# Two more column tiles as seven block products, with block sums made by GpSimd

## The chip, the cores and the metric

The kernel runs on one core of a Trainium2 chip. The metric is the device time of one execution in microseconds (us); less is better. TensorE is called PE here, VectorE DVE, ScalarE ACT, GpSimd POOL and SyncE SP, as in the profile.

## What is computed

Attention with a soft cap on its scores (2 batches, 12 heads, 448 positions, head size 64), and behind it two feed-forward blocks on 896 tokens of 768 numbers:

```python
x = _moe_ref(x=x, **moe_kwargs)      # h = x @ w_in; h * softmax(h), normalised, @ w_out
# and the second block, which the change is about:
g = x @ w_gate                       # 768 -> 1536
silu = g * (1.0 / (1.0 + np.exp(-g)))
val = x @ w_val                      # 768 -> 1536
return (silu * val @ w_out).astype(np.float32)
```

All is float32. TensorE multiplies rounded parts: each matrix is split into hi (rounded) and lo (the rest), and a product is three matmuls, hi x hi, hi x lo and lo x hi (`mm3`). The split is one ACT copy (hi) and one DVE subtraction (lo); a split of a bank in PSUM reads that bank twice.

## The kernel before

The stages follow each other on TensorE: attention, h (first block's first product), x (its second product, `ff1_x2`), the gate and value products (`ff2_gv`, `ff2_gv_seven`), and the output product (`ff2_out`).

The x stage makes six columns j of 128 model features for 896 tokens. Columns 0 and 1 are made in token blocks of 384, 256 and 256, columns 2 to 5 in blocks of 384 and 512. Each block's PSUM bank is split into `self.x2[j]` (hi and lo), and copied by ACT once more, as float32, into `self.xf` (line 582). Beside it w_out is converted column by column in two halves (`load_w_out`, lines 553 to 563): a DMA brings 64-bit raw words, ACT takes the absolute value, DVE clamps, shifts and merges in four steps, ACT scales by g_ln in four steps and makes hi, DVE makes lo. The first three steps of a half (absolute value, clamp, shift) are held in program order. Three w_out columns, two raw buffers and two float32 buffers exist at a time.

The gate and value stage runs over 12 column tiles fc of 128 features. A plain tile (`ff2_gv`) makes gate and value for 384 and then 512 tokens, 72 matmuls in all. A seven-product tile (`ff2_gv_seven`) takes gate and value weights, halved along the model features, as the four blocks of a 2 x 2 matrix, x halved along features and tokens as the other, and makes the product in seven block products of nine matmuls 448 wide in place of eight: 63 matmuls. It needs sums of weight blocks (`sum_steps`: two on POOL, two on DVE, and their splits) and sums of x blocks (`x_sums`, T1 to T4, split into `self.T`). Before, tiles 2 to 5 are of this kind (line 1036); `x_sums` runs in tiles 0 and 1, one of its four sums behind each half (line 1058), a subtraction 1344 wide on DVE and a split.

In a seven-product tile the products are, in order: A11 (bank g), S2 with T2 (b), A12 (on top of g), S3 with T3 (on top of b), S1 with T1 (c), A22 with T4 (e), S4 (on top of c). ACT copies bank g to `p1` after the first product, and the third may write g only after that. At the end come the multiplications of the results with silu, and `S1f`, `S3f`, `A11` and `A61`, which the output stage reads (lines 706 to 712).

Weights are kept in four buffers `self.g4` and in `self.w1`; plain tiles use two of them in turn. Raw loads go out on SP's queue, with two raw and two float32 buffers in the `st` pool. TensorE keeps program order throughout; from the x stage to the end of the gate and value stage the other engines' instructions are ordered by a planner when the kernel is built, and PE's are pinned. `early` (line 1034) says in which tile which part of the second w_out is loaded.

Of the kernel before, what the change touches and what calls it, by code (L numbers as in the profile page):

```python
# [5 lines left out]
F32 = mybir.dt.float32  # L6
# [4 lines left out]
AF = mybir.ActivationFunctionType  # L11
ALU = mybir.AluOpType
# [25 lines left out]
class Kernel:  # L38
# [526 lines left out]
    def ff1_x2(self, j, get, N, o):  # L565

        st = {}

        def part(a, z):
            def f():  # L570
                l, w = get(), self.wos[j]
                if a == 0:
                    st["ps"] = self.pt.tile([128, 512], F32, name=f"x2_{j}_{o}", tag="m")[:, :N]
                ps = st["ps"]
                for fc in range(a, z):
                    self.mm3(ps, (w[:, 0, fc, :], w[:, 1, fc, :]), (l[:, fc, 0, :], l[:, fc, 1, :]),
                             fc == 0, fc == self.K1 - 1)
                if z == self.K1:
                    hi, lo = self.x2[j][:, 0, o:o + N], self.x2[j][:, 1, o:o + N]
                    self.hi_act(hi, ps)  # L580
                    self.lo_dve(lo, ps, hi)
                    self.A.activation(self.xf[:, j, o:o + N], ps, AF.Copy)
            return (3 * (z - a) * N / 2400, f)

        c = self.K1 // 2
        return [part(0, c), part(c, self.K1)]


    def load_gv(self, fc, i):

        if fc not in self.gvs:
            self.gvs[fc] = [self.g4[(fc % 2) * 2 + n].rearrange("p (u k f) -> p u k f", u=2, f=128) for n in range(2)]
        n, w, d = "gv"[i], (self.w_gate, self.w_val)[i], self.gvs[fc][i]
        src = w[:, fc * 128:(fc + 1) * 128].rearrange("(k p) f -> p k f", p=128)
        f = self.f32_shifted(self.load_shifted(src, f"w{n}_{fc}"), f"w{n}_{fc}").rearrange("p (k f) -> p k f", k=self.KD)
        self.hi_act(d[:, 0], f)
        self.lo_dve(d[:, 1], f, d[:, 0])
# [24 lines left out]

    def x_sums(self, i):

        x = [self.xf[:, 3 * (m // 2):3 * (m // 2) + 3, 448 * (m % 2):448 * (m % 2) + 448] for m in range(4)]
        d, p, m, t = ((0, 1, 0, 0), (1, 3, 1, 2), (3, 3, 0, 1), (2, 2, 3, 3))[i]
        self.V.tensor_tensor(x[d], x[p], x[m], op=ALU.subtract)
        self.split([self.T[t][:, u] for u in range(2)], x[d])

    def sum_steps(self, fc):  # L630

# [29 lines left out]
    def ff2_gv_seven(self, fc):  # L661

        V, add, mult = self.V, ALU.add, ALU.mult
        n, k, ee = self.HN, fc, self.ee
        a, s24, s31, a22 = self.gvs[fc]
        half = lambda t, h: t.rearrange("p (h u k f) -> p h u k f", h=2, u=2, k=3)[:, h]
        A11, A12, S2, S4, S3, S1 = (half(t, h) for t in (a, s24, s31) for h in range(2))
        A22 = a22.rearrange("p u (k f) -> p u k f", k=3)
        X = lambda kh, th: [[self.x2[3 * kh + c][:, u, 448 * th:448 * th + 448] for u in range(2)] for c in range(3)]
        T1, T2, T3, T4 = ([[t[:, u, c] for u in range(2)] for c in range(3)] for t in self.T)  # L670
        bank = lambda m: self.pt.tile([128, 512], F32, name=f"{m}_{fc}", tag="m")[:, :448]

        def product(acc, w, x, start):
            for c in range(3):
                self.mm3(acc, (w[:, 0, c], w[:, 1, c]), x[c], start and c == 0, c == 2, not start)

        sg, c22, p1, u2 = (ee[:, 448 * m:448 * m + 448] for m in range(4))
        last = fc + 1 == self.KD
        first, second, third = (lambda: None,) * 3 if last else self.sum_steps(fc + 1)
        if last:  # L680
            self.load_gv(fc + 1, 1)
        a = bank("g")
        product(a, A11, X(0, 0), True)
        self.A.activation(p1, a, AF.Copy)
        b = bank("b")
        product(b, S2, T2, True)
        V.tensor_tensor(u2, p1, b, op=add)
        product(a, A12, X(1, 0), False)
        self.A.activation(sg, a, AF.Silu)
        first()  # L690
        if last:
            self.load_gv(fc + 1, 0)
        product(b, S3, T3, False)
        V.tensor_tensor(p1, p1, b, op=add)
        c = bank("c")
        product(c, S1, T1, True)
        V.tensor_tensor(c22, p1, c, op=add)
        second()
        e = bank("e")
        product(e, A22, T4, True)  # L700
        V.tensor_tensor(p1, p1, e, op=add)
        third()
        product(c, S4, X(1, 1), False)
        V.tensor_tensor(u2, u2, c, op=add)
        self.A.activation(u2, u2, AF.Silu)
        V.tensor_tensor(p1[:, :n], p1[:, :n], sg[:, :n], op=mult)
        V.tensor_tensor(self.S1f[:, k, :64], p1[:, n:], sg[:, n:], op=mult)
        self.split(self.A11[k], p1[:, :n])
        V.tensor_tensor(self.S1f[:, k, 64:], c22[:, :320], u2[:, :320], op=mult)
        V.tensor_tensor(c22[:, 320:], c22[:, 320:], u2[:, 320:], op=mult)  # L710
        V.tensor_tensor(self.S3f[:, k], p1[:, :n], self.S1f[:, k], op=ALU.subtract)
        self.split(self.A61[k], c22[:, 320:])

    def split(self, d, src):
# [212 lines left out]
    def run(self):  # L927
        nc = self.nc
        KD, K1, K2, F1 = self.KD, self.K1, self.K2, self.F1
# [16 lines left out]
        w = [self.w_in_steps(i) for i in range(KD)]  # L946
        f, g, hi, lo = zip(*w)
# [47 lines left out]
        n = self.HN = self.DM // 2  # L995
# [35 lines left out]
        self.sg = (self.ee[:, :n], self.ee[:, n:n + 512])  # L1031
        self.T1f = [self.ee[:, n + 512 + n * i:n + 512 + n * (i + 1)] for i in range(3)] + [t1, self.sms]
        self.t1 = t1
        early = {6: (6, 8), 7: (0, 1), 8: (2, 3), 9: (4,)}
        for fc in range(K2):
            if 2 <= fc < KD:
                self.ff2_gv_seven(fc)
                continue
            if fc == KD:
                w8 = self.w8 = wb.tile([128, 8, 2, n], F32R, name="w8", tag="w8")  # L1040
                w = both(w8) + [(w1[:, 0], w1[:, 1])]
                w += [p for g in self.g4[:2] for p in both(g.rearrange("p (k u n) -> p k u n", k=2, u=2))]
                self.B11, self.B21 = w[4:10], w[:4] + w[10:12]
            for i, (N, o) in enumerate(((n, 0), (512, n))):
                if fc == 1:
                    if i == 0:
                        first, second, third = self.sum_steps(2)
                        first()
                elif fc + 1 < K2:
                    self.load_gv(fc + 1, i)  # L1050
                elif i == 0:
                    self.load_w2(5)
                    self.load_w2(10)
                for c in early.get(fc, ())[i:i + 1]:
                    self.load_w2(c)
                self.ff2_gv(fc, N, o)
                if fc < 2:
                    self.x_sums(2 * fc + i)
            if fc == 1:
                second()  # L1060
                third()


        self.pinned = None
# [42 lines left out]
```

## Time and profile before

| | us |
|---|---|
| median of 3 runs (486.08 to 486.86) | 486.66 |
| the profiled execution | 486.02 |
| its span | 484.2 |
| PE busy | 474.9 |
| DVE busy | 371.7 |
| ACT busy | 303.3 |
| POOL busy | 29.5 |

The span is the time from the first to the last instruction that the profile shows; the execution's own time is 1.8 us longer. Matmuls are pipelined, so that rows of consecutive ones overlap by some tenths of a microsecond: the distance from one row's start to the next one's is the time that it costs. A note in square brackets is the idle time of the engine ahead of an instruction, and what ended it.

### The profile page before, as it was taken

Reading aid. Unit: us, or ns where it says so; the run is one execution under the profiler, and the core shown is the slowest. Engines: PE = TensorE matmul, PEld = TensorE weight load, DVE = VectorE, ACT = ScalarE, POOL = GpSimd, SP = SyncE. Lnnn points to the kernel's source line nnn. Section 1 sums busy time; section 2 is a strip of 40 time slices with the busy share of each in tenths; the row PEclk is TensorE's granted clock in tenths of the full one; section 3 lists DMA queues with packets and bytes.
Section 4 is the critical chain, followed back from the end, with each engine's and each line's share of the span. In section 5 each row is a group of like instructions: output and inputs, shape, how many; then the busy total and the mean of one; then the engine's idle time right before and its main releaser. Section 6 shows DMA issues by size and latency. Waiting matters only on the chain.

```text
span 484.2 us, 7694 instructions
## 1 busy us (share of the span) xinstructions
PE 474.9 (98%) x3006; PEld 390.4 (81%) x3006; DVE 371.7 (77%) x626; ACT 303.3 (63%) x440; POOL 29.5 (6%) x70
## 2 busy tenths in 40 slices
PE   9999999999999997999999999999999999999997
PEld 7445454548888897988998988899988899999996
DVE  3689999986779976475798878877567526999991
ACT  5999999931244787558976666777677616335220
POOL 1020101031000000000003011000000000000000
PEclk9999999999999998999999999999999999999999
DMA  6886565002001214126444234665566601010012
GB/s 184 206 209 153 123 174 146 20 2 87 1 0 43 88 45 111 65 72 208 131 130 137 72 119 130 195 195 186 168 231 197 195 1 49 17 57 10 18 53 93
DMA packets 65060, 52.34 MB, mean 108 GB/s; under 512 B 35584, under 2 KB 61952, under 8 KB 64256
## 3 DMA queue, kind: packets, MB, share of 16 engines
q1 hardware_dynamic: 64992, 51.86, 36.2%
q8 instruction: 23, 0.38, 0.3%
q14 instruction: 13, 0.11, 0.1%
q0 software_dynamic: 32, 0.00, 0.0%
HBM read 49.10 MB, written 2.75 MB: 107 GB/s over the span
## 4 chain that ended last, share of the span: by engine, by line
PE 93%; DVE 4%; ACT 2%; issue 1%; ACTq 0%
PE p L30 16%; PE g L30 14%; PE h L30 12%; PE v L30 12%; PE x L30 12%; PE pv L30 8%; PE sc L30 7%; PE S L30 4%; PE b L30 2%; PE c L30 2%; PE lt L30 1%; PE T L30 1%; PE warm L30 1%; DVE wo L30 1%; PE e L30 1%
## 5 line engine op out<-in xcount | busy, mean ns | idle before, releaser
L30 PE MATMUL g<-x,g 128*128 128x384 f32 (+2 forms) x360 | 77.0, 365 | 1.7 <-ACT ee L30 1.7
L30 PEld LDWEIGHTS g<-x,g 128*128 128x128 f32 x360 | 65.6, 188 | 9.8 <-ACT ee L30 2.8
L30 PE MATMUL v<-x,g 128*128 128x512 f32 (+1 forms) x288 | 60.2, 362 | 0.0
L30 PE MATMUL h<-wi,x 128*128 128x512 f32 x252 | 59.2, 393 | 0.0
L30 PEld LDWEIGHTS v<-x,g 128*128 128x128 f32 x288 | 52.1, 188 | 5.6
L30 PEld LDWEIGHTS h<-wi,x 128*128 128x128 f32 x252 | 46.8, 188 | 11.2 <-issue 1.5
L30 ACT ACTIVATE P<-sc,consts 112x896 f32<-112x896 f32 x48 | 45.3, 1009 | 3.8 <-PE sc L30 2.2
L30 ACT ACTIVATE P<-P,consts 112x3584 f32<-112x3584 f32 (+1 forms) x13 | 39.7, 3061 | 0.1
L30 PE MATMUL pv<-P,v 112*32 112x448 f32 x384 | 38.5, 540 | 0.0
L30 PEld LDWEIGHTS sc<-ks 64*112 64x112 f32 x288 | 23.3, 171 | 18.3 <-issue 8.4
L30 PE MATMUL sc<-ks 64*112 64x448 f32 x288 | 35.9, 379 | 0.2
L30 PE MATMUL x<-lB,wo 128*128 128x256 f32 (+1 forms) x192 | 35.2, 337 | 0.0
L30 PE MATMUL x<-lA,wo 128*128 128x384 f32 x144 | 29.5, 354 | 3.2 <-ACT wo L30 2.9
L30 PEld LDWEIGHTS x<-lB,wo 128*128 128x128 f32 x192 | 29.6, 189 | 3.4
L30 PEld LDWEIGHTS pv<-P,v 112*32 112x32 f32 x384 | 12.2, 110 | 22.9 <-issue 20.9
L30 PEld LDWEIGHTS x<-lA,wo 128*128 128x128 f32 x144 | 26.4, 198 | 5.0 <-ACT wo L30 3.4
L30 ACT ACTIVATE ee<-h,sms 128x512 f32<-128x512 f32 x14 | 9.5, 681 | 33.2 <-DVE sms L30 33.2
L30 PE MATMUL p<-w,a 128*128 128x384 f32 x144 | 26.8, 334 | 0.0
L30 PEld LDWEIGHTS p<-w,a 128*128 128x128 f32 x144 | 25.2, 188 | 0.1
L30 DVE TENSOR_TENSOR x<-x,x 128x448 fp32r<-128x448 f32 (+3 forms) x26 | 15.3, 587 | 10.6 <-ACT x L30 10.1
L30 DVE TENSOR_TENSOR g<-wg,g 128x768 fp32r<-128x768 f32 x16 | 15.3, 956 | 10.0 <-ACT g L30 9.3
L30 PE MATMUL S<-P,ones 112*32 112x448 f32 x192 | 22.4, 549 | 0.0
(201 smaller groups left out, 857.5 us busy)
## 6 DMA issues: line engine op xcount, KB each, us to landing
wg_raw<-in_moe_w_gate_dram SPq DMA_DIRECT2D x12, 765.8 KB, 4.2
wv_raw<-in_moe_w_val_dram SPq DMA_DIRECT2D x12, 765.8 KB, 4.2
wi_raw<-in_moe_w_in_dram SPq DMA_DIRECT2D x6, 1024.0 KB, 5.6
wo_raw<-in_moe_w_out_dram SPq DMA_DIRECT2D x12, 512.0 KB, 3.4
w_raw<-in_moe_w_out_dram SPq DMA_DIRECT2D x6, 767.6 KB, 4.2
v<-in_v_dram SPq DMA_DIRECT2D x24, 112.0 KB, 3.7
kq<-in_k_dram SPq DMA_DIRECT2D x22, 112.0 KB, 2.8
kq<-in_q_dram SPq DMA_DIRECT2D x22, 112.0 KB, 2.8
```

The lines of the kernel that those rows point to most:

```text
L30: i = f(*a, **k)
```

## The change

Tiles 1 to 6 are made as seven products in place of tiles 2 to 5. Tile 6 is the first whose results go on top of those of the first six (`A12`, `A22`, added to `S1f`), so its end is written out separately. Since tile 1 needs the x sums, they are made earlier: ACT no longer copies x's banks to `xf`; POOL adds hi and lo of a column when the column is complete (from column 2 on, which does columns 0 to 2), and makes the four block sums in pieces of 448, three for column 2 and three for each of columns 3 to 5. The splits (`x_split`) all run in tile 0, as do the weight sums of tile 1. In the tail of a seven-product tile the first product with silu is written to `S3f` rather than in place, and the 128-wide multiplication and S3's subtraction go to POOL. Tile 0 uses other weight buffers, tile 7's gate weight is loaded two products later within the last seven-product tile, and the loads of `early` and the `w8` buffer come one tile later.

```diff
@@ ff1_x2
-                    self.A.activation(self.xf[:, j, o:o + N], ps, AF.Copy)
+                    if o + N == 896 and j > 1:
+                        for m in range(3) if j == 2 else (j,):
+                            x = self.x2[m].bitcast(F32)
+                            self.G.tensor_tensor(self.xf[:, m], x[:, 0], x[:, 1], op=ALU.add)
+                        self.x_sums(j - 2)
@@ load_gv
-            self.gvs[fc] = [self.g4[(fc % 2) * 2 + n].rearrange("p (u k f) -> p u k f", u=2, f=128) for n in range(2)]
+            self.gvs[fc] = [self.g4[m].rearrange("p (u k f) -> p u k f", u=2, f=128)
+                            for m in (((0, 1), (2, 3))[fc % 2] if fc else (2, 1))]
@@ x_sums
-        x = [self.xf[:, 3 * (m // 2):3 * (m // 2) + 3, 448 * (m % 2):448 * (m % 2) + 448] for m in range(4)]
-        d, p, m, t = ((0, 1, 0, 0), (1, 3, 1, 2), (3, 3, 0, 1), (2, 2, 3, 3))[i]
-        self.V.tensor_tensor(x[d], x[p], x[m], op=ALU.subtract)
-        self.split([self.T[t][:, u] for u in range(2)], x[d])
+        c = i - 1
+        x = [self.xf[:, k + 3 * (m // 2), 448 * (m % 2):448 * (m % 2) + 448] for m in range(4) for k in range(3)]
+        x = [x[3 * m:3 * m + 3] for m in range(4)]
+        if i == 0:
+            todo = [(0, 1, 0, k) for k in range(3)]
+        else:
+            todo = [(1, 3, 1, c), (3, 3, 0, c), (2, 2, 3, c)]
+        for d, p, m, k in todo:
+            self.G.tensor_tensor(x[d][k], x[p][k], x[m][k], op=ALU.subtract)
+
+    def x_split(self, i):
+
+        d = (0, 3, 1, 2)[i]
+        src = self.xf[:, 3 * (d // 2):3 * (d // 2) + 3, 448 * (d % 2):448 * (d % 2) + 448]
+        self.split([self.T[i][:, u] for u in range(2)], src)
@@ ff2_gv_seven
-        n, k, ee = self.HN, fc, self.ee
+        n, k, ee = self.HN, fc % self.KD, self.ee
-        last = fc + 1 == self.KD
+        last = fc == self.KD
...
-        if last:
-            self.load_gv(fc + 1, 0)
         product(b, S3, T3, False)
         V.tensor_tensor(p1, p1, b, op=add)
         c = bank("c")
         product(c, S1, T1, True)
         V.tensor_tensor(c22, p1, c, op=add)
         second()
+        if last:
+            self.load_gv(fc + 1, 0)
...
-        V.tensor_tensor(p1[:, :n], p1[:, :n], sg[:, :n], op=mult)
+        G = self.G
+        if last:
+            V.tensor_tensor(p1, p1, sg, op=mult)
+            V.tensor_tensor(c22, c22, u2, op=mult)
+            self.split(self.A12[k], p1[:, :n])
+            V.tensor_tensor(self.S1f[:, k, :64], self.S1f[:, k, :64], p1[:, n:], op=add)
+            V.tensor_tensor(self.S1f[:, k, 64:], self.S1f[:, k, 64:], c22[:, :320], op=add)
+            for w, src in ((slice(0, 64), p1[:, n:]), (slice(64, 512), c22)):
+                self.split([p[:, w] for p in self.A22[k]], src)
+            return
+        V.tensor_tensor(self.S3f[:, k], p1[:, :n], sg[:, :n], op=mult)
         V.tensor_tensor(self.S1f[:, k, :64], p1[:, n:], sg[:, n:], op=mult)
-        self.split(self.A11[k], p1[:, :n])
+        self.split(self.A11[k], self.S3f[:, k])
         V.tensor_tensor(self.S1f[:, k, 64:], c22[:, :320], u2[:, :320], op=mult)
-        V.tensor_tensor(c22[:, 320:], c22[:, 320:], u2[:, 320:], op=mult)
-        V.tensor_tensor(self.S3f[:, k], p1[:, :n], self.S1f[:, k], op=ALU.subtract)
+        G.tensor_tensor(c22[:, 320:], c22[:, 320:], u2[:, 320:], op=mult)
+        G.tensor_tensor(self.S3f[:, k], self.S3f[:, k], self.S1f[:, k], op=ALU.subtract)
         self.split(self.A61[k], c22[:, 320:])
@@ run
-        early = {6: (6, 8), 7: (0, 1), 8: (2, 3), 9: (4,)}
+        early = {7: (6, 8), 8: (0, 1), 9: (2, 3), 10: (4,)}
         for fc in range(K2):
-            if 2 <= fc < KD:
+            if 1 <= fc <= KD:
                 self.ff2_gv_seven(fc)
                 continue
-            if fc == KD:
+            if fc == KD + 1:
...
-                if fc == 1:
+                if fc == 0:
                     if i == 0:
-                        first, second, third = self.sum_steps(2)
+                        first, second, third = self.sum_steps(1)
                         first()
+                        self.x_split(1)
+                    else:
+                        self.x_split(2)
...
-                if fc < 2:
-                    self.x_sums(2 * fc + i)
-            if fc == 1:
+            if fc == 0:
                 second()
+                self.x_split(0)
                 third()
+                self.x_split(3)
```

## Rows read from the trace of the kernel before

**Rows 1.** The page: PE's share, then two groups of instructions (line engine op, names).

```profile
PE 474.9 (98%) x3006; PEld 390.4 (81%) x3006; DVE 371.7 (77%) x626; ACT 303.3 (63%) x440; POOL 29.5 (6%) x70
...
L30 PE MATMUL g<-x,g 128*128 128x384 f32 (+2 forms) x360 | 77.0, 365 | 1.7 <-ACT ee L30 1.7
...
L30 DVE TENSOR_TENSOR g<-wg,g 128x768 fp32r<-128x768 f32 x16 | 15.3, 956 | 10.0 <-ACT g L30 9.3
```

**Rows 2.** Busy time by window (us), PEclk granted clock, then DMA: two plain tiles.

```profile
233.00:247.50 14.50, 14.50 (x73) 13.03 (x73) 13.18 (x13) 14.22 (x19) 0.00 (x0) 1.00 0.51 155
...
315.80:330.20 14.40, 14.40 (x73) 13.00 (x72) 9.50 (x18) 12.16 (x20) 0.00 (x0) 1.00 0.58 179
```

**Rows 3.** PE's timeline (start us, us, instructions), gate and value stage.

```profile
233.04 3.31 PE L30 MATMUL g<-x,g 128*128 128x384 f32 x18
...
247.51 3.31 PE L30 MATMUL g<-x,g 128*128 128x384 f32 x18
...
261.97 1.99 PE L30 MATMUL g<-x,g 128*128 128x448 f32 x9
...
274.74 1.99 PE L30 MATMUL g<-x,g 128*128 128x448 f32 x9
...
279.06 2.12 PE L30 MATMUL g<-x,g 128*128 128x448 f32 x9 [0.51 <-ACT ee L30]
...
315.77 3.31 PE L30 MATMUL g<-x,g 128*128 128x384 f32 x18
```

**Rows 4.** Timeline of DVE and ACT ahead of the gap at 279.06.

```profile
277.80 0.55 DVE L30 TENSOR_TENSOR s<-ee,s 128x384 f32<-128x384 f32 x1
...
278.46 0.54 ACT L30 ACTIVATE ee<-g 128x448 f32<-128x448 f32 x1 [0.23 <-DVE s L30]
```

**Rows 5.** Timeline of POOL and DVE: POOL's two-input steps and one DVE step.

```profile
129.75 0.55 POOL L30 TENSOR_TENSOR sms<-sms,consts 128x1 f32<-128x1 f32 x1 [8.80 <-DVE sms L30]
...
253.78 1.41 POOL L30 TENSOR_TENSOR t<-wv 128x384 f32<-128x384 f32 x1 [76.06 <-DVE wv L30]
...
254.23 1.38 DVE L30 TENSOR_TENSOR w<-wv,w 128x384 fp32r<-128x384 f32 x1
...
279.30 1.02 POOL L30 TENSOR_TENSOR t<-wv 128x384 f32<-128x384 f32 x1 [12.79 <-DVE wv L30]
```

**Rows 6.** Timeline of DVE and PE, second half of the x stage.

```profile
205.09 1.56 DVE L30 TENSOR_TENSOR xf<-xf 128x1344 f32<-128x1344 f32 x1 [0.66 <-ACT xf L30]
206.57 0.88 DVE L30 TENSOR_SCALAR wo<-wo 128x512 f32<-128x512 f32 x2
207.48 1.42 DVE L30 SCALAR_TENSOR_TENSOR wo<-wo_raw,wo 128x512 uint32<-128x512 uint32 x2
...
211.14 0.69 DVE L30 TENSOR_TENSOR wo<-wo,wo 128x512 fp32r<-128x512 f32 x1
...
218.39 2.03 PE L30 MATMUL x<-lA,wo 128*128 128x384 f32 x10 [0.25 <-DVE wo L30]
...
223.02 2.27 PE L30 MATMUL x<-lA,wo 128*128 128x384 f32 x12
...
227.89 2.55 PE L30 MATMUL x<-lA,wo 128*128 128x384 f32 x12
...
234.37 0.68 DVE L30 TENSOR_TENSOR x<-x,x 128x512 fp32r<-128x512 f32 x1
```

**Rows 7.** Instructions on the tile xf (count: duration ns min/median/max, first and last start).

```profile
L30 ACT ACTIVATE xf<-x x14: 381/480/606, 174.1 to 237.0; 128x384 f32<-128x384 f32 x6, 128x256 f32<-128x256 f32 x4, 128x512 f32<-128x512 f32 x4
L30 DVE TENSOR_TENSOR xf<-xf x4: 1549/1552/1557, 205.1 to 245.4; 128x1344 f32<-128x1344 f32 x4
```

**Rows 8.** Timeline of POOL and DVE at the end of the attention stage.

```profile
106.45 3.27 POOL L30 COPY sm<-tr 32x14 f32<-32x14 f32 x4 [4.87 <-DVE tr L30]
107.47 0.69 DVE L30 CAST wi<-wi 128x1024 fp32r<-128x1024 f32 x1
108.19 1.23 DVE L30 TENSOR_TENSOR wi<-wi,wi 128x1024 fp32r<-128x1024 f32 x1
```

## What I predict

> **What bounds the kernel now.** I read the engines' shares on the page first, then the busy time by stage, then TensorE's timeline through the stage that is changed, and last what its few gaps wait for. TensorE (PE) is busy for 474.9 of 484.2 us [rows 1]. The reader is to see that it is full in the changed stage as well: in a plain column tile PE fills the whole window while VectorE (DVE) and ScalarE (ACT) are busy for 13.2 and 14.2 of 14.5 us in the first tile, less in later ones [rows 2]. So the time is matmul work, plus those places where weights, sums or buffers come late. Three such gaps lie in the seven-product tiles, 1.7 us in all [rows 1], the first at 279.06 with 0.51 [rows 3]; two small ones lie in the x stage before it, at 218.39 and 227.89, where PE waits for w_out (wo) conversion [rows 6].
>
> **Two more seven-product tiles.** A plain tile takes 247.51 - 233.04 = 14.47 us; the first seven-product tile, which does not stall, takes 274.74 - 261.97 = 12.77 [rows 3]. Tiles 1 and 6 change from one kind to the other: 2 x (14.47 - 12.77) = **-3.4 us**. PE was granted full clock (1.00) in the windows of both ends of the stage [rows 2], so columns saved are time saved.
>
> **The stalls at the third product.** The four seven-product tiles take 315.77 - 261.97 = 53.80 us, 2.72 more than 4 x 12.77 [rows 3]. In each of the last three the third product writes the bank that ACT copies to p1 first, and that copy starts late: at 278.46, just after DVE's S3 subtraction, which ran from 277.80 to 278.35 (0.55 us) and was the last reader of the old p1 [rows 4]. After the change p1's last readers are two multiplications ahead of it (S3f takes the product itself), and the subtraction and the 128-wide multiplication go to GpSimd (POOL). Bounds: nothing is won if the copy stays behind the A61 steps on ACT, now fed by POOL; all is won if it runs when its product ends. I take all, **-2.7 us**, since the copy's inputs are then ready 1.8 us before PE needs it. POOL needs about 1.0 us for the 384-wide step [rows 5] and its consumer is the output stage, long after; DVE gets rid of 0.55 us and a shorter step a tile.
>
> **The block sums on POOL during x.** Removed: 14 ACT copies to xf of 0.48 us, 6.7 in all, and four DVE subtractions of 1.55, 6.2 in all [rows 7], none of which PE waits for directly. Added: six additions 896 wide and twelve subtractions 448 wide on POOL. No row has these widths. A 384-wide one takes 1.02 us alone [rows 5]; in proportion the new ones take 2.38 and 1.19 us. If a fixed 0.55 us, the time of a one-element POOL instruction at 129.75 [rows 5], lay in it, they would take 1.65 and 1.10. I take 2.2 and 1.17, nearer to the upper end since the row is the same operation: 6 x 2.2 + 12 x 1.17 = 27 us, 5.7 us in each x column of about 10 us.
>
> The Trainium skill, GPSIMD Engine Reference, section 3.1, gives some 2.6 cycles an element for this operation; an estimate from it and the 384-wide row is 2.1 us for the wide additions, which would lower the 27 us by about half a microsecond.
>
> POOL itself has time, but the port it shares with DVE has not. At 254.23 a DVE lo step of 384 elements took 1.38 us beside a POOL step instead of 0.55; it ended at 255.61, its own time after POOL had ended at 255.19 and a little [rows 4, 5]. And POOL gets in between two DVE steps: from 106.45 four small copies needed 3.27 us, while DVE ran a CAST and a lo step one after the other; the last copy ended 0.3 us after them [rows 8]. So a DVE step with all operands in SBUF can wait for one whole POOL step each time.
>
> Such steps are just what the wo conversions consist of: each half of a 128-column block has two clamp and shift steps (0.88), two merge steps (1.42) and one lo step (0.69), 2.99 us [rows 6]. They are already as late as they may be: for the second half of columns 4 and 5 PE waits at 218.39 and, inside the 2.55 us at 227.89 (2.27 for the same twelve matmuls at 223.02), again [rows 6].
>
> Bound from below: the port works without a gap. From 204.5 to the last lo step of column 5 it has four halves (12.0), the first gate weight's merge and lo (1.9) and POOL's third and fourth addition with six subtractions (11.4): 25.3 us, so 229.8, where PE wanted it at 227.6; some 2.2 us, and 3 if not every hole is filled. If POOL's steps fell only into DVE's idle time the cost would be 0, and the two waits (0.25 and 0.28 us) would go too. Bound from above: the order of before is kept on each engine. Then, from the end of column 2, half 4a's shift waits 2.2 us for the third addition and both merges 1.1 for subtractions; what the removed DVE subtraction at 205.09 gives back (1.56) doesn't cover that, and lo of 4a ends at 214.1 instead of 211.8 [rows 6], PE needing it at 212.6 (1.5 us lost). Half 4b starts behind it on ACT, waits 2.2 us for the fourth addition, and its lo stands behind four steps of 5a, each held 1.1: 225.0 against 219.0 (6.0 lost). Half 5b loses 2.4 more. Together 9.9, less the 0.5 of waits already there, some 9 us. Only the first three steps of a half are held in program order, the planner may reorder the rest, and with 2 us of DVE work gone it has cause to: I take **+3.0 us** and keep 0 to 9.
>
> **The first seven-product tile.** All conversions for it now lie in tile 0. From the last x column's lo (it ends at 235.05, 2.0 us into the tile [rows 3, 6]) POOL has an addition, three subtractions and the two weight sums: 2.2 + 3.5 + 2.0 = 7.7 us, with up to five DVE steps of 0.96 [rows 1] between: 12.5. Two weight subtractions (1.1, as wide as that of [rows 4]), hi and lo (0.96 each, hi taken as long as lo) follow: 2.0 + 12.5 + 3.0 = 17.5 us, where the second product wants S2 at 14.47 + 1.82 = 16.3. Late by 1.2, or not at all with fewer interleaved steps; up to 3 if two of the four x splits (1344 wide, as the subtraction of 1.55 us [rows 7]) stand ahead of p1's copy. I take **+0.5 us**.
>
> **Moved at no cost.** Weights of tile 1 come through the same two SP loads. The last seven-product tile loads tile 7's gate weight into the buffer of S1 and S3, free after the fifth product: hi and lo (1.9) have two products, 3.65 us. The w_out loads of the output stage move by one tile each; a tile with two of them and the next weights, at 315.8, left PE without a gap [rows 2].
>
> **Sum.** -3.4 - 2.7 + 3.0 + 0.5 = -2.6 us. The profiled execution took 486.02 us (span 484.2 and 1.8 around it) and becomes 483.4; the median of before, 486.66, stands 0.64 above it, so I forecast **484.0**.
>
> **Rivals.** *The port decides (slower).* The planner does not know of the shared port, so the order stays and the x stage loses 9 us, the first tile 1: -6.1 + 10 = +4, about 490.6. For it: the held step at 254.23 and the two waits for wo. Against: only three steps of a half are fixed. It decides from 6 us of loss in the x stage on. The Trainium skill, SBUF — State Buffer, section "SBUF: two separate sides", says that the shared pair is an exclusive lock held for the whole instruction; this case's trace agrees with 1.38 us instead of 0.55 for a 384-wide lo step, and no row shows it beside an 896-wide one.
>
> *Hidden.* POOL's steps fall into holes of DVE, wo is as early as before or earlier: -6.1 + 0.5 = -5.6, about 481. For it: ACT and DVE lose 6.7 and 6.2 us of work around here. Against: 5.7 us of POOL and 6 of wo steps on one port in each 10 us column.
>
> *The stalls stay.* p1's copy remains behind the A61 step, which now waits for POOL's multiplication: -3.4 + 3.0 + 0.5 = +0.1, about 486.7. Against: the copy no longer depends on these steps.
>
> **Chances.** 0.37 for the forecast (482.4 to 485.6), 0.20 for hidden (480.5 to 482.4), 0.15 for within 0.2% of before (a measurement of this kernel can tell about that much, 1 us), 0.28 for the port. So faster 0.57, same 0.15, slower 0.28. The range holds the hidden case and most of the port's: 480.5 to 490.0.
>
> **What would show it.** PE's gaps at column 4 and 5 of the x stage, released by wo, say whether 0, 3 or 9 us went there; DVE's wo steps must show 1 to 2 us more beside POOL's. Tiles 1 to 6 should start 12.8 us apart with no gap at the third product; a gap there released by ACT's p1 copy makes the second term wrong. A gap at the second or fourth product of tile 1 prices the fourth. Additions of much less than 1.65 or more than 2.4 us, or DVE steps that run undisturbed beside them, would make the prediction wrong at its root.

## The result, and the profile after

The changed kernel takes 490.16 us (median of 5 runs, 489.69 to 492.38) against 486.66 in the same session: 1.0085 times the time of before, 95% interval 1.0058 to 1.0111. It is slower by 3.5 us. The forecast was 484.0 with a range up to 490.0; what came is close to the rival called "the port decides", forecast at 490.6 with a chance of 0.28. Its sum agrees better than its parts do, as the section on the prediction shows.

The changed kernel's page, engines' busy time and the group of x matmuls (engine, op, names, count, busy, mean ns, idle before them):

```profile
PE 474.3 (97%) x2988; PEld 389.4 (80%) x2988; DVE 392.7 (80%) x635; ACT 302.1 (62%) x435; POOL 77.9 (16%) x102
...
L30 PE MATMUL x<-lA,wo 128*128 128x384 f32 x144 | 29.7, 355 | 6.6 <-DVE wo L30 6.0
```

DVE is busy for 21 us more than before [rows 1] with nine instructions more, although four subtractions of 1.55 us have left it. The run without the sums, below, has the same 635 DVE instructions and 375.0 us of them, so 17.7 of the 21 us are steps that take longer while POOL makes the sums.

PE's timeline of the changed kernel, from the middle of the x stage to tile 7 (start us, us, instructions, idle before):

```profile
184.98 8.66 PE L30 MATMUL x<-lB,wo 128*128 128x256 f32 x60
...
208.74 2.73 PE L30 MATMUL x<-lA,wo 128*128 128x384 f32 x12 [0.51 <-ACT wo L30]
...
219.86 3.57 PE L30 MATMUL x<-lA,wo 128*128 128x384 f32 x10 [5.21 <-DVE wo L30]
...
232.39 2.01 PE L30 MATMUL x<-lA,wo 128*128 128x384 f32 x10 [0.80 <-DVE wo L30]
...
237.00 3.31 PE L30 MATMUL g<-x,g 128*128 128x384 f32 x18
...
251.47 1.99 PE L30 MATMUL g<-x,g 128*128 128x448 f32 x9
257.28 0.68 PE L30 MATMUL b<-a,g 128*128 128x448 f32 x2 [3.83 <-ACT g L30]
258.28 2.98 PE L30 MATMUL b<-a,g 128*128 128x448 f32 x7 [0.32 <-DVE g L30]
...
270.46 2.02 PE L30 MATMUL g<-x,g 128*128 128x448 f32 x9
...
322.54 2.02 PE L30 MATMUL g<-x,g 128*128 128x448 f32 x9
...
335.56 3.29 PE L30 MATMUL g<-x,g 128*128 128x384 f32 x18
```

Three rows of the kernel before that the prediction did not show: the gap of 2.90 us at 185.77, where PE waits for ACT's step on wo, with the twelve matmuls behind it, which took 3.94 us where twelve others took 2.27; the 60 matmuls in the middle of the x stage; and the start of tile 7:

```profile
185.77 3.94 PE L30 MATMUL x<-lA,wo 128*128 128x384 f32 x12 [2.90 <-ACT wo L30]
189.55 8.66 PE L30 MATMUL x<-lB,wo 128*128 128x256 f32 x60
...
330.24 3.31 PE L30 MATMUL g<-x,g 128*128 128x384 f32 x18
```

Starts of stages in both traces [rows 3] give the balance:

| stretch | before | after | difference |
|---|---|---|---|
| start to the 60 matmuls in the middle of x | 189.55 | 184.98 | -4.6 |
| from there to tile 0 | 43.49 | 52.02 | +8.5 |
| tile 0 | 14.47 | 14.47 | 0 |
| tile 1 | 14.46 | 18.99 | +4.5 |
| tiles 2 to 5 | 53.80 | 52.08 | -1.7 |
| tile 6 | 14.47 | 13.02 | -1.5 |
| rest | 153.96 | 153.94 | 0 |

Together +5.3 us, the difference of the spans (489.5 and 484.2). The profiled execution was one of the slower ones of its kernel: profiled again, the span was 486.7 us, and the last section shows 1.3 of the 2.8 us between them.

Now the cause. DVE's and POOL's timelines of the changed kernel ahead of the gap of 5.21 us:

```profile
212.52 2.68 DVE L30 TENSOR_SCALAR wo<-wo 128x512 f32<-128x512 f32 x2
215.24 3.03 DVE L30 SCALAR_TENSOR_TENSOR wo<-wo_raw,wo 128x512 uint32<-128x512 uint32 x2
218.19 1.61 DVE L30 TENSOR_TENSOR wo<-wo,wo 128x512 fp32r<-128x512 f32 x1
...
212.68 2.23 POOL L30 TENSOR_TENSOR xf<-x 128x896 f32<-128x896 f32 x1 [7.25 <-DVE x L30]
215.00 4.26 POOL L30 TENSOR_TENSOR xf<-xf 128x448 f32<-128x448 f32 x3
```

The reader is to see two chains that take turns. Clamp and shift of half 5a take 2.68 us in place of 0.88, its two merges 3.03 in place of 1.42, the lo step of 4b behind them 1.61 in place of 0.69 [rows 6], each lengthened while POOL has a step running. PE starts again at 219.86, when that lo step ends (219.80). The order on DVE is the one of before: 4b's lo stands behind 5a's four steps. The planner did not move it; from the 60 matmuls to tile 0 the order of DVE's steps is also the same as in the run without the sums.

Not every DVE step is held. Those that were lengthened (wo, weights, x splits) go from SBUF to SBUF. The lo steps of x, which read a PSUM bank, took 0.41 to 0.70 us throughout (185 to 260); few of them fell beside a POOL step here, but in the run in pieces, below, two did (at 218.26 and 228.59) and took 0.54 and 0.56 us.

The same in tile 0, on DVE: the x splits and the weight steps ahead of tile 1.

```profile
239.05 3.11 DVE L30 TENSOR_TENSOR a<-xf,a 128x1344 fp32r<-128x1344 f32 x1 [0.52 <-ACT a L30]
242.08 1.91 DVE L30 TENSOR_TENSOR g<-wg,g 128x768 fp32r<-128x768 f32 x1
243.91 1.91 DVE L30 SCALAR_TENSOR_TENSOR wv<-wv_raw,wv 128x768 uint32<-128x768 uint32 x1
...
246.21 2.19 DVE L30 TENSOR_TENSOR a<-xf,a 128x1344 fp32r<-128x1344 f32 x1
248.32 1.51 DVE L30 TENSOR_TENSOR w<-wv,w 128x384 fp32r<-128x384 f32 x1
249.76 2.37 DVE L30 TENSOR_TENSOR a<-xf,a 128x1344 fp32r<-128x1344 f32 x1
...
252.52 0.55 DVE L30 TENSOR_TENSOR wg<-t,wg 128x384 f32<-128x384 f32 x1
...
255.40 0.54 DVE L30 TENSOR_TENSOR wg<-wg 128x384 f32<-128x384 f32 x1
```

Alone these steps take 1.55, 0.96, 0.96, 1.55, 0.55 and 1.55 us, so six of them were held for 5.9 us. The first weight subtraction, for which S2 waits, runs at 252.52, after tile 1 has begun; hi and lo of S2 follow the second at 255.40, and PE waits for them.

After the long gaps PE is slow for a while. Busy time by window around the gap of 5.21 us (us; PE, PEld, DVE, ACT, POOL, then PE's granted clock, DMA):

```profile
213.00:219.00 6.00, 1.65 (x8) 0.98 (x6) 5.93 (x4) 1.65 (x6) 5.76 (x4) 0.82 0.28 87
219.00:225.00 6.00, 5.14 (x17) 4.83 (x18) 3.27 (x6) 3.28 (x7) 0.26 (x1) 0.61 0.40 131
225.00:231.00 6.00, 6.00 (x31) 5.28 (x30) 4.52 (x6) 4.04 (x9) 3.10 (x2) 1.00 0.66 219
```

Behind the gap the granted clock is 0.61 on the mean, so largely at the lower of its two levels (1.2 GHz), and 1.00 (2.4 GHz) again from 225: ten matmuls take 3.57 us there, 2.01 behind the short gap at 232.39. Behind tile 1's gap it is 0.66 (257 to 262), and in the kernel before, around the gap of 2.90 us, 0.66 as well (185 to 190).

### The profile page after: what moved, and what is told of

It reads as the page before. It is cut to its first block, busy times and chain, and to the rows that moved or that the text cites. A ratio compares the mean times of both kernels' runs of the same rounds, so it can differ in the third digit from the quotient of the medians.

```text
span 489.5 us, 7697 instructions
## 1 busy us (share of the span) xinstructions
PE 474.3 (97%) x2988; PEld 389.4 (80%) x2988; DVE 392.7 (80%) x635; ACT 302.1 (62%) x435; POOL 77.9 (16%) x102
## 4 chain that ended last, share of the span: by engine, by line
PE 90%; DVE 6%; ACT 2%; issue 1%; DVEq 0%
PE p L30 16%; PE g L30 13%; PE h L30 12%; PE v L30 9%; PE pv L30 7%; PE sc L30 7%; PE x L30 6%; PE b L30 5%; PE c L30 5%; DVE wo L30 4%; PE S L30 4%; PE e L30 2%; PE lt L30 1%; ACT wo L30 1%; PE T L30 1%; PE warm L30 1%
## 5 line engine op out<-in xcount | busy, mean ns | idle before, releaser
L30 PE MATMUL g<-x,g 128*128 128x384 f32 (+2 forms) x324 | 69.8, 365 | 0.0
L30 PEld LDWEIGHTS g<-x,g 128*128 128x128 f32 x324 | 59.7, 188 | 6.5
L30 PE MATMUL v<-x,g 128*128 128x384 f32 (+1 forms) x216 | 45.1, 362 | 0.0
L30 PEld LDWEIGHTS v<-x,g 128*128 128x128 f32 x216 | 39.1, 188 | 4.2
L30 PE MATMUL b<-a,g 128*128 128x448 f32 x108 | 25.9, 384 | 4.1 <-ACT g L30 3.8
L30 POOL COPY sm<-tr 32x14 f32<-32x14 f32 x48 | 14.8, 309 | 92.6 <-DVE tr L30 91.1
L30 ACT ACTIVATE wo<-wo,gt 128x128 f32<-128x128 f32 x48 | 15.3, 393 | 19.7 <-DVE wo L30 19.7
L30 PEld LDWEIGHTS b<-a,g 128*128 128x128 f32 x108 | 21.0, 197 | 7.0 <-ACT g L30 4.2
```

The costliest lines, as they stand in the source:

```text
L30: i = f(*a, **k)
```

## The experiments

All run beside the kernel before, whose median was 486.6 to 486.9 us. The theory is that POOL's steps hold DVE's steps at the port that they share; its rival is that the work itself, or its order, is too much for tile 0 and the x stage.

**Without the sums.**

```diff
-                    if o + N == 896 and j > 1:
...
-                        self.x_sums(j - 2)
...
+        self.G.memset(self.xf, 0.5)
```

The constant is written once, at 166.8 us of the profile, as the x stage begins.

> The changed kernel without the eighteen additions and block sums (left out: xf is filled with a constant once, so T1 to T4 are not the sums of x). Port theory (POOL's steps hold DVE's w_out and weight steps, in the x stage and in tile 0): the waits for wo in columns 4 and 5 go (8.5 us between 193.5 and 237.0 fall to under 1), DVE's 5.9 us of held time in tile 0 go and with them most of tile 1's gap of 4.2 us; about 476 to 478. Work theory (tile 0 holds more conversions than ACT and DVE can do, and the x stage is late by the planner's order): tile 1's gap stays at 3 us or more and wo is late as well; 484 to 487.

476.34 us, ratio 0.980 (0.976 to 0.984). PE has no gap in the x stage, which from the 60 matmuls on takes 42.56 us (185.62 to 228.18) in place of 52.02: **the sums on POOL cost 9.5 us there**. In tile 1 a gap of 1.0 us is left:

```profile
242.64 1.99 PE L30 MATMUL g<-x,g 128*128 128x448 f32 x9
245.26 0.68 PE L30 MATMUL b<-a,g 128*128 128x448 f32 x2 [0.63 <-ACT g L30]
246.25 1.68 PE L30 MATMUL b<-a,g 128*128 128x448 f32 x7 [0.32 <-DVE g L30]
...
256.89 1.99 PE L30 MATMUL g<-x,g 128*128 128x448 f32 x9
```

Tile 1 takes 14.25 us, 1.5 above 12.77: that part is left without any sums, so with the other work of tile 0 alone; the other 4.7 us of the 6.2 come with the sums. In this run the splits wait for no sum and run first in tile 0, so the 4.7 us hold two things: DVE's steps held beside POOL, and sums that come late.

The page of this run, to be set beside that of the changed kernel:

```profile
PE 469.3 (99%) x2988; PEld 387.3 (82%) x2988; DVE 375.0 (79%) x635; ACT 302.1 (64%) x435; POOL 49.7 (10%) x85
```

**The same steps on DVE.**

```diff
-                            self.G.tensor_tensor(self.xf[:, m], x[:, 0], x[:, 1], op=ALU.add)
+                            self.V.tensor_tensor(self.xf[:, m], x[:, 0], x[:, 1], op=ALU.add)
-            self.G.tensor_tensor(x[d][k], x[p][k], x[m][k], op=ALU.subtract)
+            self.V.tensor_tensor(x[d][k], x[p][k], x[m][k], op=ALU.subtract)
```

> The changed kernel with the same eighteen steps on DVE in place of POOL: no shared port, but some 14 us more of DVE work. Port theory: no step of DVE runs longer than without POOL, columns 4 and 5 lose less than the 6.5 us of idle that they lost on POOL, 484 to 488 in all. Work theory: DVE has still more to do, so wo and tile 1 come later than in the changed kernel, above 491.

485.13 us, ratio 0.9968 (0.9952 to 0.9985): 5 us faster than on POOL, and 1.5 faster than before. Instructions on wo (ns min/median/max), first of the changed kernel (193 to 237), then of this one (193 to 235):

```profile
L30 DVE SCALAR_TENSOR_TENSOR wo<-wo_raw,wo x10: 680/1096/2489, 194.2 to 225.2; 128x512 uint32<-128x512 uint32 x10
L30 DVE TENSOR_TENSOR wo<-wo,wo x6: 691/1154/1639, 191.6 to 230.7; 128x512 fp32r<-128x512 f32 x6
```

```profile
L30 DVE SCALAR_TENSOR_TENSOR wo<-wo_raw,wo x10: 682/684/693, 194.4 to 224.6; 128x512 uint32<-128x512 uint32 x10
L30 DVE TENSOR_TENSOR wo<-wo,wo x5: 682/693/693, 198.6 to 227.3; 128x512 fp32r<-128x512 f32 x5
```

With the additions on DVE no wo step is held, and an addition takes 1.08 us where POOL takes 2.18. The work costs time here too: from the 60 matmuls on the x stage takes 48.72 us, 6.2 more than without sums, and tile 1 15.86, 1.6 more. So the work is no small matter; on POOL it cost 9.5 and 4.7.

**The tail alone.**

```diff
-        V.tensor_tensor(p1[:, :n], p1[:, :n], sg[:, :n], op=mult)
+        V.tensor_tensor(self.S3f[:, k], p1[:, :n], sg[:, :n], op=mult)
...
+        G.tensor_tensor(self.S3f[:, k], self.S3f[:, k], self.S1f[:, k], op=ALU.subtract)
```

> The kernel before with the changed tail alone (S3f written directly, the short multiplication and S3's subtraction on POOL). Tiles 2 to 5 lose their three gaps: 1.7 us of idle, with the matmuls behind them 2.7; 484.0 to 485.0. Rival: the copy of p1 stays late or the port holds DVE in the tail; within 0.5 us of before.

484.13 us, ratio 0.9954 (0.9935 to 0.9973), 2.5 us less. Tiles 2 to 5 run from 262.79 to 313.86 without a gap, 51.07 us or four times 12.77. In tile 3 the copy of bank g runs at 277.87, when its product ends and ahead of A61's step on ACT at 279.12; PE wants the bank at 279.20. (In tile 3 of the kernel before, which starts 0.82 us earlier, it ran at 278.46 [rows 4].)

```profile
277.87 0.53 ACT L30 ACTIVATE ee<-g 128x448 f32<-128x448 f32 x1
...
279.12 0.29 ACT L30 ACTIVATE a<-ee 128x128 fp32r<-128x128 f32 x1
```

**xf by POOL, block sums on DVE in tiles 0 and 1.** The kernel before, with the change's additions in place of ACT's copies.

> The kernel before with xf made by six POOL additions in place of ACT's copies, block sums still on DVE in tiles 0 and 1. Both theories: the gap of 2.9 us at 185.8 goes, since ACT is free of the copies of columns 0 and 1 (about 4.5 us up to the middle of column 2). Port theory: 13 us of POOL beside wo gives back 2 to 4 us in columns 4 and 5; 483 to 485. Work theory: nothing is given back; 482.

483.5 us, ratio 0.9936 (0.9919 to 0.9953). The gap at 185.77 is gone; the 60 matmuls start at 184.40, 5.2 us earlier, and from there to tile 0 it takes 45.46 us, 2.0 more than before. Two waits for wo are longer (1.49 and 0.86 us).

**ACT's copies kept, only the block sums on POOL.** Otherwise the changed kernel.

> The changed kernel with ACT's fourteen copies to xf kept as before and only the twelve block sums on POOL (some 15 us instead of 28). Port theory: POOL holds DVE half as long; the loss from the middle of column 2 to the end of the x stage falls from 9.5 us (against the run without sums) to 3 to 6, tile 1 gains about 1 us; but the gap at 185 for wo, 4.5 us with what follows, comes back; 487 to 491 in all. If instead ACT's relief was what moved the planner's order and cost columns 4 and 5 their waits, these waits go altogether and the time falls under 485.

490.86 us, ratio 1.0087 (1.0056 to 1.0117). The gap of 2.90 us at 185.83 is back. From the 60 matmuls on the x stage takes 47.99 us, 4.5 more than before, about as the theory says; tile 1 did not gain (19.52 us), against what was expected of it.

**One tile more, nothing in x.** Tiles 2 to 6 as seven products, the changed tail, sums and copies as before.

> Tiles 2 to 6 as seven products (one more than before), with the changed tail; x sums and copies as in the kernel before, DVE in tiles 0 and 1, no POOL in the x stage. Port theory: the second and third term of the prediction stand by themselves, 486.6 - 1.7 - 2.7 = 482.2 (481.5 to 483). Rival (seven-product tiles behind tile 5 cost more than 12.8 us by the late gate weight of tile 7): a gap at tile 7, 483.5 to 485.

482.34 us, ratio 0.9907 (0.9887 to 0.9926): 4.5 us less, as the prediction's first two terms give for one tile and the stalls (1.7 + 2.7). Tile 7 follows tile 6 after 12.77 us.

**The same, and columns 0 and 1 added by POOL.**

```diff
-                    self.A.activation(self.xf[:, j, o:o + N], ps, AF.Copy)
+                    if j > 1:
+                        self.A.activation(self.xf[:, j, o:o + N], ps, AF.Copy)
+                    elif o + N == 896:
+                        x = self.x2[j].bitcast(F32)
+                        self.G.tensor_tensor(self.xf[:, j], x[:, 0], x[:, 1], op=ALU.add)
```

> As the run with tiles 2 to 6, and xf of columns 0 and 1 made by two POOL additions in place of ACT's six copies; columns 2 to 5 are copied by ACT. Port theory: two additions (4.4 us of POOL around 189 and 194) fall where wo has 7 us of slack, so only ACT's gap at 185 goes, 4.5 us with what follows: 477 to 479. Rival (any POOL step in the x stage is given back by wo in columns 4 and 5): 481 or more.

**477.25 us, ratio 0.9806 (0.9787 to 0.9825)**: 9.6 us faster than the kernel before. The 60 matmuls start at 184.96, tile 0 at 228.52, 43.56 us later, as long as before: two additions early, where wo has slack, cost nothing, and what ACT no longer does is won.

**The POOL work in pieces.** The changed kernel with additions and sums 224 wide.

> The changed kernel with the same POOL work in pieces 224 wide (24 for the additions, 24 for the block sums, some 33 us of POOL in place of 28). If a DVE step waits for one whole POOL step at a time, its waits fall from 1.2 to 2.2 us to under 0.7 and the x stage loses 4 to 6 us instead of 9.5: 485 to 488. If what counts is POOL's total time on the port, it loses as much or more: 490 to 492.

483.55 us, ratio 0.9930 (0.9905 to 0.9954), 6.6 us less than in whole steps, a larger gain than was expected. From the 60 matmuls on the x stage takes 43.42 us, 0.9 more than without sums; PE waits 0.58 us for wo. The merges of wo take 1.04 us by the median, 1.05 at most, where whole steps made it 2.49. POOL was busy for 30.1 us of this stretch, 24.2 in the changed kernel (184.98 to 237.00), yet DVE's total is 383.4 us in place of 392.7. So in the x stage how long one POOL step is counts more than how much there is in all. The pieces also begin earlier, the first at 174.2 in place of 189.0; what that alone is worth was not measured.

Tile 1 keeps its gap (4.97 us), and the port theory alone does not explain it: DVE's steps in tile 0 were held for some 3.9 us in place of 5.9. POOL itself was later. S2's first step overwrites weights that POOL's second weight sum reads, so it has to come behind that sum, which ended 16.3 us into tile 0, in the changed kernel 13.7.

**POOL steps that nobody reads.** The 477.3 us kernel with twelve POOL steps behind columns 2 to 4, into a tile that is free there.

```diff
+                        if o + N == 896 and j < 5:
+                            x = self.x2[j].bitcast(F32)
+                            self.G.tensor_tensor(self.ee[:, :896], x[:, 0], x[:, 1], op=ALU.add)
+                            for m in range(3):
+                                self.G.tensor_tensor(self.ee[:, 1024:1472], x[:, 0, :448], x[:, 0, 448:], op=ALU.subtract)
```

> The 477.3 us kernel with twelve POOL steps that nobody reads, put where the changed kernel has its own for columns 2, 3 and 4 (one addition 896 wide and three subtractions 448 wide behind each, 17 us in all, into a tile that is free there). No instruction of another engine waits for their results before tile 0. Port theory: DVE's wo steps are held as in the changed kernel and PE waits for wo in columns 4 and 5: 5 to 9 us, 482 to 486. Rival (what cost time was what depends on the sums, or the planner's order without the copies): unchanged, 477 to 478.

487.97 us, ratio 1.0026 (1.0012 to 1.0040): 10.7 us lost to steps without a reader, more than was expected. The loss lies in the x stage, 53.91 us from the 60 matmuls (184.36) to tile 0 (238.27):

```profile
210.46 3.66 PE L30 MATMUL x<-lA,wo 128*128 128x384 f32 x12 [2.84 <-ACT wo L30]
...
218.20 0.62 PE L30 MATMUL x<-lA,wo 128*128 128x384 f32 x2 [0.67 <-ACT wo L30]
...
220.85 2.50 PE L30 MATMUL x<-lA,wo 128*128 128x384 f32 x10 [2.03 <-DVE wo L30]
...
233.66 2.00 PE L30 MATMUL x<-lA,wo 128*128 128x384 f32 x10 [1.25 <-DVE wo L30]
```

No result is awaited there, and ACT does its copies of these columns as before. The rival that the planner chose a worse order is out too: from the 60 matmuls to tile 0 DVE's and ACT's steps stand in the same order in both traces. DVE has the same 630 instructions, and they take 10.5 us longer; the pages of the 477.3 us kernel and of this run:

```profile
PE 470.4 (99%) x2997; PEld 387.9 (82%) x2997; DVE 378.8 (80%) x630; ACT 303.4 (64%) x439; POOL 44.9 (9%) x82
```

```profile
PE 473.6 (98%) x2997; PEld 390.1 (80%) x2997; DVE 389.3 (80%) x630; ACT 303.9 (63%) x439; POOL 64.8 (13%) x94
```

What is left as the way from POOL to PE is DVE's held steps. This decides between theory and rival for the x stage.

**The last column's sums on DVE, and the changed kernel again.**

> The changed kernel with the last column's addition and three block sums on DVE, the others on POOL. The x stage keeps its loss of 9.5 us. Port theory of tile 1: in tile 0 DVE does 2.9 us more but is held 4 to 5 us less, so the gap of 4.2 us before the second product falls to 1 to 3: 487 to 489. Work theory of tile 1: DVE has more to do there, the gap grows by up to 2.9: 491 to 493.

> The changed kernel once more, beside the two others: 489.5 to 491.5. Its products of nine matmuls were 1.86 us apart in all seven-product tiles, 1.82 in the kernel before outside one tile. If that spacing belongs to the kernel it comes again; if it is a matter of chance in one execution, it is 1.82 in some tiles and the span is 1.3 us shorter.

488.53 us (ratio 1.0045, 1.0025 to 1.0066) and 490.88 (1.0078, 1.0052 to 1.0103). Beside each other: with three sums and an addition moved from POOL to DVE, the gaps before and in the second product of tile 1 fall from 3.83 and 0.32 us to 1.42 and 1.31, although DVE has more to do:

```profile
254.76 0.68 PE L30 MATMUL b<-a,g 128*128 128x448 f32 x2 [1.42 <-ACT g L30]
256.75 2.21 PE L30 MATMUL b<-a,g 128*128 128x448 f32 x7 [1.31 <-DVE g L30]
```

So the longer gap that the work theory forecast is out. But the move does two things at once: DVE is held less, and POOL is free sooner, so that its second weight sum ends 10.7 us into tile 0 in place of 13.7. How much of tile 1's 4.7 us is the held steps and how much the lateness of POOL's own steps stays open.

## Why the prediction was wrong

The step that failed is the third term: the block sums in x were put at +3.0 us because the planner would reorder DVE's steps around POOL's. It did not, and the stretch behind the 60 matmuls lost 8.5 us. The fourth term was too small as well (6.2 in place of 0.5), and a gain of 4.6 us had no term. With the two terms that held, the measured parts are -3.4 - 2.7 + 8.5 + 6.2 - 4.6 = +4.0; the medians differ by 3.5.

**Two more tiles, -3.4: right.** Tile 6 takes 12.77 us in the run with one more tile; in the profiled execution of the changed kernel 13.02, by the spacing shown in the last section. Tile 1 would have been the same without its gap.

**The stalls, -2.7: right.** The tail alone gave -2.5 in the median and -2.7 in the profile's tiles 2 to 5, and no gap at the third product is left in any run that has it. Its rival, that the copy stays behind A61's steps, is out: the copy runs when its product ends.

**The block sums in x, +3.0 with 0 to 9: the value taken was wrong, the mechanism right.** The sums cost 9.5 us against the run without them and 8.5 against before, where the upper bound was 9. The sentence that failed is that the planner has cause to reorder. It left 4b's lo behind 5a's four steps, as the upper bound assumed, and kept the order that it makes without the sums. An order was in the rows, a better one was a hope. The upper bound's places were right and its delays too long: PE waited 0.51, 5.21 and 0.80 us where it had 1.5, 6.0 and 2.4. The matmuls behind these waits took 2.3 us more than elsewhere, 1.8 of it at the lower clock behind the longest one; the prediction had no term for that. Durations were right: 2.13 to 2.23 us for an addition (2.2 taken), 1.19 at the least for a block sum (1.17 taken). The port's price was read from the row at 254.23 a little too high: that step ended 0.42 us after POOL's, not its own 0.55.

**"None of which PE waits for directly": wrong.** ACT's copies did cost PE time: those of columns 0 and 1 stood among wo's steps on ACT, and the gap of 2.90 us at 185.77, with the slow matmuls behind it, went with them, -4.6 us. The kernel before, on ACT just ahead of that gap:

```profile
184.81 0.39 ACT L30 ACTIVATE xf<-x 128x256 f32<-128x256 f32 x1
185.07 0.65 ACT L30 ACTIVATE wo<-wo 128x512 fp32r<-128x512 f32 x1
```

In the 477.3 us kernel, which differs from the one with tiles 2 to 6 by these copies alone, the same hi step of wo runs at 180.82. The planner also put other steps earlier there, so the copies' own time and the order that came of it are not told apart. The gap stood in the profile of before as the longest wait of PE; I took it as no part of the change, since the sums' own place was later. So the x stage came out at +3.9 altogether, near the forecast +3.0, by two errors of opposite sign: that is luck.

**The first seven-product tile, +0.5 with 0 to 3: mis-sized.** It lost 6.2 us against 12.77. The walk let POOL's steps wait for DVE's but counted no time by which DVE's own six steps are held (5.9 us), and it put the weight subtractions at once behind POOL's sums, where DVE's order had two splits and other steps ahead of them. 1.5 us of it stay without any sums; how the rest divides between held steps and late sums is open, as said above.

**The rivals.** "The port decides" had the mechanism of the x stage. That its 490.6 agrees with the 490.16 measured is luck in part: it had x at +9 and the first tile at +1; x lost 8.5 and tile 1 6.2, and the 4.6 us from ACT made up for it. "Hidden" has nothing for it with whole steps: those that nobody reads show that they don't fall into holes of DVE. The Trainium skill, SBUF — State Buffer, section "SBUF: two separate sides", calls the pair that DVE and GpSimd share an exclusive lock held for a whole instruction. The runs agree, with 2.68 us for two 0.44 us steps beside one addition, and with the gain from pieces. A chance of 0.28 for a case whose mechanism and order stood in the rows was too low.

## What to carry to other kernels

Before GpSimd is given work, count which DVE steps from SBUF to SBUF run beside it and what they feed: in this kernel each could wait for a whole GpSimd step. Two long GpSimd steps where that chain had slack cost nothing here, and short ones cost 0.9 us in the x stage; long ones beside the chain without slack cost 9.5, more than the same work on DVE (6.2). Where nothing shows that a planner takes such a cost into account, forecast with the order that the trace shows. And read the longest wait of the critical engine in the whole stage, even where the change seems to touch only its end: work taken from ACT paid there, and the parts that stood up on their own gave 477.25 us.

## What was not expected of the hardware

Products of nine matmuls 448 wide follow each other by 1.82 us in some executions and 1.86 in others. PE's timeline of the changed kernel, run again:

```profile
259.76 1.99 PE L30 MATMUL g<-x,g 128*128 128x448 f32 x9
261.59 1.99 PE L30 MATMUL b<-a,g 128*128 128x448 f32 x9
263.41 1.98 PE L30 MATMUL c<-a,g 128*128 128x448 f32 x9
```

and as it was profiled first, at the same place of tile 1:

```profile
261.06 2.12 PE L30 MATMUL g<-x,g 128*128 128x448 f32 x9
263.02 2.02 PE L30 MATMUL b<-a,g 128*128 128x448 f32 x9
264.88 2.02 PE L30 MATMUL c<-a,g 128*128 128x448 f32 x9
```

In each of these two executions all of tiles 2 to 6 kept the one or the other spacing (12.77 or 13.02 us a tile, 1.3 us in five), at a granted clock of 1.00 in both (262 to 335 and 260 to 333). Five of the thirteen profiled executions show 1.86 in some or all of their seven-product tiles. From tile to tile it changed only behind gaps, in the kernel before too: 1.86 behind the gap at 279.06, 1.82 again behind that at 292.67. What sets it stays open.
